# Chunked attention and a token/channel mixer on one core: batch 1's attention placed anew beside batch 0's feed-forward stage, with a subtracting softmax for every batch

## The chip, the cores and the metric

The kernel runs on one core of a Trainium2 chip. TensorE (PE) does the matrix products and transposes, VectorE (DVE) and ScalarE (ACT) read its results from eight PSUM banks, GpSimd (POOL) does small memsets and copies, and SyncE (SP) issues every DMA. The metric is the device time of one execution in microseconds, lower is better.

## What is computed

Shapes: 4 batches, 8 heads, 768 tokens, head dimension 64, 8 memory tokens, chunks of 32 queries that see 16 keys to the left and 8 to the right; rank 32, model width 512, hidden width 2048.

```python
for c in range(S // 32):                               # chunked attention
    k_full = concat(mem_k, k[l_start:r_end]); v_full = concat(mem_v, v[l_start:r_end])
    scores = scale * q_c @ k_full.T
    a = exp(scores - max(scores)); a = a / (sum(a) + 1e-9)
    out[c] = a @ v_full
x = out.transpose(0, 2, 1, 3).reshape(B, S, 512)
u = x + (x.T @ U @ V).T                                # low-rank token mixing
y = u + relu(u @ w_ch1) @ w_ch2                        # feed-forward over channels
```

The parameters U, V, w_ch1 and w_ch2 arrive as float64 and are decoded on the chip into a high and a low float32r part.

## The kernel before, in words

**Stages.** Batch 0's attention runs first, alone, while the weights begin to arrive. Then come the feed-forward stages of batches 0, 1, 2 and 3. Beside the stage of batch b runs the attention of batch b + 1, in pieces that are placed between the feed-forward's steps.

**The feed-forward.** A batch has 6 token tiles of 128, in two blocks of three, and the hidden width has 16 slices f. One unit is a block and a slice: `w1_step` is 12 matmuls of 128x384 (high weights by high u, low by high, high by low), followed by ACT's relu into `hh` and DVE's remainder `hl` (line 964); `w2_step` is 9 matmuls of 128x512 into three accumulators, the last three of which read `hl`. A batch thus has 32 units. In `both_blocks` (batch 0, lines 1019 to 1070) the two blocks take turns over the first `SPLIT` = 11 slices (units 0 to 21), since the weights are still being decoded; units 22 to 26 are block 0's slices 11 to 15, units 27 to 31 block 1's. Unit 26 ends with DVE's additions into `x` and the three stores of block 0 (line 973), unit 31 with those of block 1. The low parts of w1 for block 1's slices are read back from DRAM (`w1l`, line 378) two units ahead, into four buffers.

**The decoding.** `stream` (line 342) decodes 32 weight chunks on ACT and DVE; `advance` moves it on, two steps a unit, or as far as the next unit's weights need. `done` counts finished chunks; it reaches 32 at the start of unit 26. Its work space is `vbs[1]`, `vbs[2]` and two slots.

**Attention of one batch.** Three pairs T = 0, 1, 2 of token tiles. The pieces are: `k_part` and `q_part` (eight transposes each and ACT's copies into `kall` or `qt`), `s_part` (128 small matmuls into two PSUM banks, then the softmax in `s_weights` and the sums in `s_sums`), `t_part` (eight transposes of the weights and ACT's copies), `av_part` (128 small matmuls with the values in `vb`, then DVE's division into `x`). After the last pair come `collect` (12 matmuls with U), the replication (line 837) with a cast and a subtraction (lines 842, 843), six products with `v3` (line 858) and DVE's additions. `make_uT` (line 933) then turns three tiles of x for the next stage. `attention` is a generator: each `yield` ends a piece, and `place(n)` issues the next n.

**Order.** PE and SP keep the order in which the program issues (`manual_schedule`); DVE does so until unit 22 and ACT until unit 2; after that, and on POOL, the scheduler orders by priority. In `both_blocks`, `place(1)` is called at unit `2 * SPLIT - SOON` = 16 and `border()` twice in each of units 23 to 31, ahead of and behind the `w1_step`; what is left goes to `following` in unit 31. In the stages of batches 1 and 2, `STEPS` says at which slice a piece is placed.

**Loads of a batch's attention.** `loads` (line 421) is a generator too: k and q of pairs 0 and 1 with the memory values (17 steps), v of pair 0 (11), k and q of pair 2 (8), v of pairs 1 and 2. `serve(3)` issues three steps a unit; `need` issues what a piece lacks. v of a pair is eight loads of 98 or 112 KB, and some edges. For batch 1, pairs 0 and 1 use `vbs[0]`, so pair 1's load waits until `av_part(0)` is issued, and pair 2 uses `vbs[1]` once `done` is 32. For batches 2 and 3 pairs 0 and 2 use `vbs[0]`, pair 1 `vbs[1]`. Raw k, q, weights, x, `qt`, `pt` and `pT` share 23 slots.

**The softmax before.** Batch 0 (lines 591 to 595, 602 to 606): maximum on DVE, subtraction on DVE into `pt`, one exponential of 128x512 on ACT, sums on DVE. Batches 1 to 3 (lines 582 to 590): q is negated and scaled when it is copied, DVE takes the minimum, and ACT does eight exponentials of 128x64 that take it as bias and give the sum by their accumulator. A pair has two halves s, each so.

PSUM has three banks `ps_a` (attention, and block 1's accumulators until unit 21), two `ps_h` and three accumulators.

Of the kernel before, what the change touches and what calls it, by code (L numbers as in the profile page):

```python
# [1 line left out]

# [6 lines left out]
F32 = mybir.dt.float32  # L9
F32R = mybir.dt.float32r  # L10
BF16 = mybir.dt.bfloat16
AF = mybir.ActivationFunctionType
# [3 lines left out]
I32 = mybir.dt.int32  # L16
U32 = mybir.dt.uint32
NEG = -3.0e38
FAR = 3.0e38
NSLOT = 23  # L20
NVE = 1
ET = mybir.EngineType
# [14 lines left out]
NDEC = 3  # L37
RATE = 2
AHEAD = 2
SOON = 6  # L40
RATEL = 3
STEPS = [0, 4, 6, 8, 9, 10, 12, 13, 14, 15, 16, 17, 18, 19, 20, 23, 25, 26, 27, 28]


@with_exitstack
def chunk_attn_then_mixer_kernel(
# [324 lines left out]
    def advance(n):  # L371
        for _ in range(n):
            next(weights, None)
# [7 lines left out]
    def attention(b, xs):  # L381
# [30 lines left out]
        def fetch_v(T):  # L412
            if T == 0:
                clear_v()
            if T == 0 or T == (2 if b == 1 else 1):
                mem_v(v_home(T))
                yield
            yield from load_v(T)
            issued.add(("v", T))

        def loads():
            for T in range(2):
                yield from fetch(T, "kn", kn, k, LEFT)
                yield from fetch(T, "qn", qn, q, 0)
                if T == 0:
                    for g in range(2):
                        nc.sync.dma_start(out=mv[64 * g:64 * g + NM].rearrange("m (j d) -> m j d", d=D), in_=mvv[b, g])
                    yield
            yield from fetch_v(0)
            yield from fetch(2, "kn", kn, k, LEFT)  # L430
            yield from fetch(2, "qn", qn, q, 0)
            for T in (1, 2):
                while (done[0] < 2 * NF if v_home(T) is vbs[1] else "av0" not in issued):
                    yield "shut"
                yield from fetch_v(T)

        def need(*what):
            while what not in issued:
                assert next(feed[0], None) != "shut"
# [11 lines left out]
                )  # L451

        def v_home(T):
            return vbs[T if b == 0 else T // 2 if b == 1 else T % 2]

        def clear_v():
            for g in range(2):
# [73 lines left out]
        def q_part(T, h):  # L531
            psv = turn(qn.pop((T, h)))
            if front[0]:
                qt = const.tile([P, 2, NB, CK], F32, name="qt", tag=f"w1_{5 + (2 * T + h) % 3}")
            else:
                qt = slot([P, 2, NB, CK], F32, "qt")
            qts[T, h] = qt
            for q_ in range(2):
                to, src = qt[:, q_].rearrange("c i (n r) -> c r i n", r=2), psv[:, q_]
                if b > 0:  # L540
                    nc.scalar.mul(out=to, in_=src, mul=-scale)
                else:
                    (nc.vector.tensor_copy if T == 0 else nc.scalar.copy)(out=to, in_=src)

# [17 lines left out]
            return banks, psv  # L562

        def s_weights(T, banks, psv):
            if b > 0:
                rs = rss[T] = sm.tile([P, 2, 2, 2, 2], F32, name="rs", bufs=3)
            far = NEG if b == 0 else FAR
            for s in range(2):
                if T == 0:
                    nc.vector.memset(psv[s][0:CK, 0, :, :, NM:NM + LEFT], far)  # L570
                if T == NP - 1:
                    nc.vector.memset(psv[s][P - CK:P, 1, :, :, NW - 8:NW], far)
                if front[0]:
                    both = const.tile([P, 2, 512], F32, name="pt", tag=f"w2_{5 + 2 * T + s}")
                    pt, pT[T, s] = both[:, 0], both[:, 1].rearrange("c (j n) -> c j n", j=4)
# [3 lines left out]
                ptv = pt.rearrange("n (a w) -> n a w", w=NW)  # L579
                mx = sm.tile([P, 8], F32, name="mx", bufs=3)  # L580
                sc = banks[s].rearrange("n (a w) -> n a w", w=NW)
                if b > 0:
                    nc.vector.tensor_reduce(out=mx, in_=sc, axis=AX.X, op=ALU.min)  # L583
                    for a in range(8):
                        t, k_, g = a // 4, a // 2 % 2, a % 2
                        nc.scalar.activation(  # L586
                            out=ptv[:, a], in_=sc[:, a], func=AF.Exp, bias=mx[:, a:a + 1], scale=-1.0,
                            accum_out=rs[:, t, g, k_, s:s + 1],
                        )
                    continue  # L590
                nc.vector.tensor_reduce(out=mx, in_=sc, axis=AX.X, op=ALU.max)
                nc.vector.tensor_tensor(
                    out=ptv, in0=sc, in1=mx[:, :, None].broadcast_to([P, 8, NW]), op=ALU.subtract,
# [1 line left out]
                nc.scalar.activation(out=pt, in_=pt, func=AF.Exp, scale=scale)  # L595

        def s_sums(T):
            if b > 0:
                rs = rss[T]
            else:  # L600
                rs = rss[T] = sm.tile([P, 2, 2, 2, 2], F32, name="rs", bufs=3)
                for s in range(2):
                    nc.vector.tensor_reduce(
                        out=rs[:, :, :, :, s].rearrange("n t g k -> n t k g"),
                        in_=pts[T, s].rearrange("n (t k g w) -> n t k g w", t=2, k=2, g=2), axis=AX.X, op=ALU.add,
                    )
            nc.vector.tensor_scalar_add(out=rs, in0=rs, scalar1=1e-9)
            nc.vector.reciprocal(out=rs, in_=rs)

        def s_part(T):  # L610
            s_weights(T, *s_turn(T))
            s_sums(T)
# [162 lines left out]
        else:  # L775
# [2 lines left out]
            feed[0] = loads()  # L778
            yield
            place_memk()  # L780
            for T in two:
                for part, name in ((k_part, "kn"), (q_part, "qn")):
                    need(name, T)
                    for h in two:
                        part(T, h)
                    yield
            s_part(0)
            yield
            for s in two:
                t_part(0, s)  # L790
            yield
            need("v", 0)
            av_part(0)
            issued.add("av0")
            yield
            need("kn", 2)
            for h in two:
                k_part(2, h)
            yield
            s_part(1)  # L800
            yield
            need("qn", 2)
            for h in two:
                q_part(2, h)
            yield
            for s in two:
                t_part(1, s)
            yield
            s_part(2)
            yield  # L810
            need("v", 1)
            av_part(1)
            yield
            for s in two:
                t_part(2, s)
            yield
            if b == 1:
                while done[0] < 2 * NF:
                    advance(1)
                    more_w()  # L820
            need("v", 2)
            av_part(2)
            yield

        if b > 0:
# [193 lines left out]
    def both_blocks(pieces, following):  # L1019
# [11 lines left out]
        for n, (blk, f, where, begins, ends) in enumerate(units):  # L1031
# [15 lines left out]
                del w1ls[f]  # L1047
            if n == 2 * SPLIT - SOON:
                place(1)
            serve(RATEL)  # L1050
            if n > 2 * SPLIT:
                border()
            hid_ = w1_step(0, blk, f, w1l)
# [18 lines left out]
    def place(n):  # L1072
        for _ in range(n):
            next(gen[0], None)

    def serve(n):
        for _ in range(n):
            if next(feed[0], "shut") == "shut":
                return

    def border():
        place(1)

    def ffn(b, blk, pieces, following):
        prev = []
# [37 lines left out]
    feed = [iter(())]  # L1123
    for b in range(B):
        gen[0] = attention(b + 1, xs) if b + 1 < B else iter(())
        pcs = [STEPS.count(n) for n in range(2 * NF)]

        def last_turns(b=b):
            for _ in gen[0]:
                pass  # L1130
            yield from make_uT(b + 1, 0)

        turns = last_turns()

# [49 lines left out]
```

## Time and profile before

| | us |
|---|---|
| median of the 3 runs | 692.09 |
| the three runs | 693.47, 688.77, 692.09 |
| the profiled execution | 689.29 |
| its span, first to last instruction | 687.5 |
| mean granted TensorE clock | 0.99 |

| stretch of the profiled execution | from, to | length |
|---|---|---|
| batch 0, units 0 to 21, from about | 60, 154.65 | 94.7 |
| batch 0, units 22 to 31, with batch 1's attention | 154.65, 234.73 | 80.1 |
| batch 1's stage, with batch 2's attention | 234.73, 392.25 | 157.5 |
| batch 2's stage, with batch 3's attention | 392.25, 549.60 | 157.4 |
| batch 3's stage | 549.60, 682.50 | 132.9 |

Times in the profile are microseconds from the start of the span, unless marked ns. A line of a timeline has the start, the length, the engine, the line of the kernel, the operation, what it writes and reads with the shape, how many, and in brackets how long the engine stood idle before and what ended that. SPq is SyncE's queue: its lines are the issues of transfers. In a line of operations by source the three durations are the least, the median and the greatest in ns. Matmuls are pipelined, so their lengths overlap: the distance from one start to the next is their cost.

### The profile page before, as it was taken

The page shows a single profiled execution, that of the slowest core. Times are in us where ns is not written, and L with a number is a line of the kernel's source. Part 1 is how long each engine was busy: PE and PEld are TensorE (multiplying, and loading weights), DVE is VectorE, ACT ScalarE, POOL GpSimd, SP SyncE. Part 2 cuts the span into 40 slices and gives each one's busy share as a digit, 9 for nine tenths or more (in the row PEclk, how much of TensorE's full clock was granted, in tenths as well). Part 3 has the DMA queues.
Part 4 walks back from the last instruction along what each step waited for, and adds up shares of the span by engine and source line. Part 5 has one row for each costly group of instructions (what it writes and reads, how often), then busy time and mean ns, then how long its engine had stood idle before and what let it go on. Part 6 is the DMA issues. An engine that isn't in the chain of part 4 may idle for free.

```text
span 687.5 us, 14945 instructions
## 1 busy us (share of the span) xinstructions
PE 658.2 (96%) x6284; PEld 576.0 (84%) x6284; DVE 246.7 (36%) x488; ACT 241.9 (35%) x792; POOL 10.1 (1%) x35
## 2 busy tenths in 40 slices
PE   7687999999879999999999999999999999999997
PEld 4457999988666799989988999898888899989996
DVE  5768666876322511132224211233223221131111
ACT  4646555677553223445211122535311111111110
POOL 2100000000000000000000000000000000000000
PEclk9999999999999999999999999999999999999999
DMA  8788444844082285427121185525220142204211
GB/s 229 165 239 298 144 154 154 251 112 129 8 218 46 87 211 127 110 60 183 48 63 50 57 225 113 145 67 154 76 63 32 30 138 67 70 23 145 65 47 46
DMA packets 122997, 79.88 MB, mean 116 GB/s; under 512 B 86994, under 2 KB 102482, under 8 KB 122930
## 3 DMA queue, kind: packets, MB, share of 16 engines
q1 hardware_dynamic: 122930, 78.93, 41.4%
q8 instruction: 49, 0.80, 0.5%
q14 instruction: 18, 0.15, 0.1%
HBM read 67.24 MB, written 10.49 MB: 113 GB/s over the span
## 4 chain that ended last, share of the span: by engine, by line
PE 86%; SPq 6%; DMA 2%; DVE 2%; ACT 2%; issue 1%; ACTq 0%; DVEq 0%
PE ps_h L957 38%; PE acc L1005 23%; PE acc L1010 12%; SPq L481 3%; PE ps_a L500 2%; PE ps_a L634 2%; PE ps_a L1005 2%; PE ps_a L557 2%; PE ps_a L941 1%; ACT pt L586 1%; PE ps_a L619 1%; PE ps_a L1010 1%; DMA rw<-in_moe_w_ch_dram 1%; PE ps_a L660 1%; DMA vb<-in_v_dram 1%
## 5 line engine op out<-in xcount | busy, mean ns | idle before, releaser
L964 DVE SCALAR_TENSOR_TENSOR hl<-ps_h,hh 128x384 fp32r<-128x384 f32 x127 | 70.7, 557 | 315.4 <-ACT hh L963 315.3
L957 PE MATMUL ps_h<-uh,w1h 128*128 128x384 f32 x508 | 174.7, 345 | 0.5 <-issue 0.5
L957 PE MATMUL ps_h<-ul,w1h 128*128 128x384 f32 x508 | 171.0, 338 | 0.0
L963 ACT ACTIVATE hh<-ps_h 128x384 fp32r<-128x384 f32 x127 | 63.2, 497 | 292.6 <-PE ps_h L957 292.6
L1005 PE MATMUL acc<-w,hh 128*128 128x512 f32 x606 | 158.4, 397 | 0.0
L1005 PEld LDWEIGHTS acc<-w,hh 128*128 128x128 f32 x606 | 111.8, 188 | 24.2 <-issue 2.5
L957 PE MATMUL ps_h<-uh,w1l 128*128 128x384 f32 x508 | 108.7, 334 | 3.4 <-DVE w1l L333 3.4
L957 PEld LDWEIGHTS ps_h<-uh,w1h 128*128 128x128 f32 x508 | 96.1, 189 | 3.8 <-issue 1.5
L957 PEld LDWEIGHTS ps_h<-ul,w1h 128*128 128x128 f32 x508 | 96.0, 189 | 2.4 <-issue 0.7
L957 PEld LDWEIGHTS ps_h<-uh,w1l 128*128 128x128 f32 x508 | 89.8, 188 | 3.7 <-DVE w1l L333 3.7
L1010 PE MATMUL acc<-w,hl 128*128 128x512 f32 x303 | 86.3, 393 | 0.0
L1010 PEld LDWEIGHTS acc<-w,hl 128*128 128x128 f32 x303 | 57.3, 189 | 12.6
L586 ACT ACTIVATE pt<-ps_a,mx 128x64 f32<-128x64 f32 x144 | 43.4, 355 | 17.3 <-DVE mx L583 15.4
L586 ACT ACTIVATION_READ_ACCUMULATOR pt<-ps_a,mx 128x1 f32 x144 | 35.6, 248 | 0.0
L521 ACT COPY kall<-ps_a 128x256 f32<-128x256 f32 x40 | 17.1, 427 | 30.8 <-PE ps_a L500 30.8
L971 DVE TENSOR_TENSOR x<-acc,x 128x512 f32<-128x512 f32 x24 | 15.2, 681 | 22.9 <-PE acc L1010 19.1
L1005 PE MATMUL acc<-w2last,hh 128*128 128x512 f32 x90 | 23.1, 392 | 0.0
L643 DVE TENSOR_TENSOR x<-ps_a,rs 128x256 f32<-128x256 f32 x44 | 15.8, 415 | 11.3 <-PE ps_a L634 9.0
L1005 PEld LDWEIGHTS acc<-w2last,hh 128*128 128x128 f32 x90 | 16.8, 188 | 3.4
L557 PEld LDWEIGHTS ps_a<-kall,qt 64*32 64x32 f32 x1344 | 16.1, 105 | 3.7 <-issue 3.3
L557 PE MATMUL ps_a<-kall,qt 64*32 64x64 f32 x1344 | 18.5, 225 | 0.2 <-issue 0.2
L1005 PE MATMUL ps_a<-w,hh 128*128 128x512 f32 x66 | 17.0, 393 | 0.0
(205 smaller groups left out, 590.7 us busy)
## 6 DMA issues: line engine op xcount, KB each, us to landing
w1l<-w1ld SPq DMA_DIRECT2D x101, 256.0 KB
rw<-in_moe_w_ch_dram SPq DMA_DIRECT2D x14, 512.0 KB
out_dram<-x SPq DMA_DIRECT2D x24, 256.0 KB
vb<-in_v_dram SPq DMA_DIRECT2D x56, 98.0 KB
raw<-in_moe_w_ch_dram SPq DMA_DIRECT2D x20, 256.0 KB
qn<-in_q_dram SPq DMA_DIRECT2D x36, 128.0 KB
rw<-in_moe_w_ch_dram SPq DMA_DIRECT2D x16, 256.0 KB
w1ld<-w1l SPq DMA_DIRECT2D x16, 256.0 KB
```

The costliest lines, as they stand in the source:

```text
L481: nc.sync.dma_start(out=vt[r0:r0 + NW - NM, n0:n1, D * j:D * j + D], in_=bass.AP(rows.tensor, rows.offset, [[step, count], [CK * step, n1 ...
L500: nc.tensor.transpose(out=psv[:, p, r, :], in_=half[:, r, 2 * p:2 * p + 2, :].rearrange("n h d -> n (h d)"), identity=ident,)
L521: copy(out=kt[:, p, :, :, m:m + w], in_=psv[:, q_])
L557: nc.tensor.matmul(out=psv[s][CK * i:CK * i + CK, t, p % 2, p // 2, :], lhsT=qt[p // 2][rows, p % 2, NI * t + i, :], rhs=kall[rows, NB * ( ...
L586: nc.scalar.activation(out=ptv[:, a], in_=sc[:, a], func=AF.Exp, bias=mx[:, a:a + 1], scale=-1.0, accum_out=rs[:, t, g, k_, s:s + 1],)
L643: nc.vector.tensor_tensor(out=x[:, 4 * D * g:4 * D * g + 4 * D].rearrange("n (j d) -> n j d", d=D), in0=psv[g][:, t], in1=rs[:, t, g].rear ...
L957: nc.tensor.matmul(out=ph[:, :TOK], lhsT=w[:, c, :], rhs=u[c], start=(m == 0), stop=(m + 1 == len(parts)),)
L963: nc.scalar.activation(out=hh, in_=ph[:, :TOK], func=AF.Relu)
L964: nc.vector.scalar_tensor_tensor(out=hl, in0=ph[:, :TOK], scalar=0.0, in1=hh.bitcast(F32), op0=ALU.max, op1=ALU.subtract,)
L971: nc.vector.tensor_tensor(out=x, in0=bank, in1=x, op=ALU.add)
L1005: nc.tensor.matmul(out=acc[tt], lhsT=h[:, sl], rhs=w, start=(begins and m == 0), stop=False,)
L1010: nc.tensor.matmul(out=acc[tt], lhsT=hl[:, sl], rhs=w2h[f], start=False, stop=ends is not None)
```

## The change

1. The softmax of batches 1 to 3 is done as batch 0's: plain copy of q, maximum, subtraction, one exponential with the scale, sums on DVE.
2. The pieces of the attention of batches 1 to 3 come in another order: scores of pair 0 right behind k of pair 1, k of pair 2 ahead of the first weighting.
3. For batch 1 the values of pair 1 go to `vbs[1]` and wait for `done` = 32; those of pair 2 go to `vbs[0]` and wait for `av_part(0)`: the way of batches 2 and 3.
4. In batch 0's stage loading starts at unit 14 (`SOON` 8), with three steps a unit until unit 21 and six (`RATES`) from unit 22.
5. The 18 borders place as `PLAN` says: one piece at each of the first 13, then 2, 1, 2, 2, 4. `make_uT(1, 0)` is chained to batch 1's attention and placed by the same list instead of by `following` in unit 31.

In the new order the borders of units 23 to 31 hold (ahead of `w1_step` / behind it): k0 / q0; k1 / s0; q1 / t0; k2 / av0; s1 / q2; t1 / s2; av1 / t2 and av2; collect / replication and three `v3` products; the other three and the first turn / the other two turns. Before they held: k0 / q0; k1 / q1; s0 / t0; av0 / k2; s1 / q2; t1 / s2; av1 / t2; av2 / collect; replication / three products, with the rest in `following`.

```diff
-FAR = 3.0e38
-SOON = 6
+SOON = 8
 RATEL = 3
+RATES = 6
+PLAN = [1] * 13 + [2, 1, 2, 2, 4, 1, 1]
...
         def fetch_v(T):
-            if T == 0 or T == (2 if b == 1 else 1):
+            if T < 2:
                 mem_v(v_home(T))
...
             for T in (1, 2):
-                while (done[0] < 2 * NF if v_home(T) is vbs[1] else "av0" not in issued):
+                while (done[0] < 2 * NF if T == 1 else "av0" not in issued):
                     yield "shut"
...
         def v_home(T):
-            return vbs[T if b == 0 else T // 2 if b == 1 else T % 2]
+            return vbs[T if b == 0 else T % 2]
...
                 if b > 0:
-                    nc.scalar.mul(out=to, in_=src, mul=-scale)
+                    nc.scalar.copy(out=to, in_=src)
...
         def s_weights(T, banks, psv):
-                if b > 0:
-                    nc.vector.tensor_reduce(out=mx, in_=sc, axis=AX.X, op=ALU.min)
-                    for a in range(8):
-                        t, k_, g = a // 4, a // 2 % 2, a % 2
-                        nc.scalar.activation(
-                            out=ptv[:, a], in_=sc[:, a], func=AF.Exp, bias=mx[:, a:a + 1], scale=-1.0,
-                            accum_out=rs[:, t, g, k_, s:s + 1],
-                        )
-                    continue
                 nc.vector.tensor_reduce(out=mx, in_=sc, axis=AX.X, op=ALU.max)
                 nc.vector.tensor_tensor(
                     out=ptv, in0=sc, in1=mx[:, :, None].broadcast_to([P, 8, NW]), op=ALU.subtract,
...
                 nc.scalar.activation(out=pt, in_=pt, func=AF.Exp, scale=scale)
...
         def s_sums(T):
-            if b > 0:
-                rs = rss[T]
-            else:
...
+            for s in range(2):
+                nc.vector.tensor_reduce(
+                    out=rs[:, :, :, :, s].rearrange("n t g k -> n t k g"),
+                    in_=pts[T, s].rearrange("n (t k g w) -> n t k g w", t=2, k=2, g=2), axis=AX.X, op=ALU.add,
+                )
...
+            for what, args in (
+                (turn_in, (k_part, "kn", 0)), (turn_in, (q_part, "qn", 0)), (turn_in, (k_part, "kn", 1)),
+                (s_part, (0,)), (turn_in, (q_part, "qn", 1)), (weights_in, (0,)), (turn_in, (k_part, "kn", 2)),
+                (weigh, (0,)), (s_part, (1,)), (turn_in, (q_part, "qn", 2)), (weights_in, (1,)), (s_part, (2,)),
+                (weigh, (1,)), (weights_in, (2,)),
+            ):
+                what(*args)
+                yield
+            weigh(2)
             yield
...
-            serve(RATEL)
+            serve(RATEL if n < 2 * SPLIT else RATES)
...
+    at = [0]
+
     def border():
-        place(1)
+        place(PLAN[at[0]])
+        at[0] += 1
...
         gen[0] = attention(b + 1, xs) if b + 1 < B else iter(())
+        if b == 0:
+            gen[0] = chain(gen[0], make_uT(1, 0))
...
         def last_turns(b=b):
             for _ in gen[0]:
                 pass
-            yield from make_uT(b + 1, 0)
+            if b > 0:
+                yield from make_uT(b + 1, 0)
```

`turn_in` needs the load and turns both halves, `weights_in` is `t_part` of both halves, `weigh` needs v and is `av_part`.

More of the change, by code (lines that the diff above doesn't have):

```diff
@@ L1 @@
 from contextlib import ExitStack
+from itertools import chain
 import concourse.bass as bass
@@ L564, in s_weights @@
         def s_weights(T, banks, psv):
-            if b > 0:
-                rs = rss[T] = sm.tile([P, 2, 2, 2, 2], F32, name="rs", bufs=3)
-            far = NEG if b == 0 else FAR
             for s in range(2):
                 if T == 0:
-                    nc.vector.memset(psv[s][0:CK, 0, :, :, NM:NM + LEFT], far)
+                    nc.vector.memset(psv[s][0:CK, 0, :, :, NM:NM + LEFT], NEG)
                 if T == NP - 1:
-                    nc.vector.memset(psv[s][P - CK:P, 1, :, :, NW - 8:NW], far)
+                    nc.vector.memset(psv[s][P - CK:P, 1, :, :, NW - 8:NW], NEG)
                 if front[0]:
@@ L597, in s_sums @@
         def s_sums(T):
-            if b > 0:
-                rs = rss[T]
-            else:
[L601 to L606, printed above, removed]
+            rs = rss[T] = sm.tile([P, 2, 2, 2, 2], F32, name="rs", bufs=3)
+            for s in range(2):
[3 more added lines that the diff above has]
+                )
             nc.vector.tensor_scalar_add(out=rs, in0=rs, scalar1=1e-9)
@@ L780, in attention, with turn_in, weigh, weights_in @@
             place_memk()
[L781 to L822, printed above, removed]
+            def turn_in(part, name, T):
+                need(name, T)
+                for h in two:
+                    part(T, h)
+            def weigh(T):
+                need("v", T)
+                av_part(T)
+                issued.add(f"av{T}")
+            def weights_in(T):
+                for s in two:
+                    t_part(T, s)
+            for what, args in (
[7 more added lines that the diff above has]
+            weigh(2)
             yield
```

## The prediction

> **What bounds the kernel now.** I read the page's busy shares first, then the windows of the stages, then TensorE's (PE's) timeline where it is not full, and last the queue that it waits for.
>
> ```profile
> span 687.5 us, 14945 instructions
> PE 658.2 (96%) x6284; PEld 576.0 (84%) x6284; DVE 246.7 (36%) x488; ACT 241.9 (35%) x792; POOL 10.1 (1%) x35
> ```
>
> The windows have, after the stretch and its length, the busy microseconds of PE, PE's weight loads, DVE, ACT and POOL, then the granted clock, the DMA share and GB/s. These four are batch 1's feed-forward stage with batch 2's attention in it, batch 2's with batch 3's, batch 3's with none, and the stretch at the end of batch 0's stage where batch 1's attention runs.
>
> ```profile
> 234.73:392.25 157.52, 157.52 (x1558) 140.48 (x1557) 39.17 (x80) 48.13 (x186) 2.03 (x6) 1.00 0.40 104
> 392.25:549.60 157.35, 157.35 (x1558) 140.35 (x1557) 39.20 (x80) 48.11 (x186) 0.61 (x2) 1.00 0.40 104
> 549.60:682.50 132.90, 132.90 (x679) 121.14 (x679) 23.21 (x42) 17.35 (x35) 0.00 (x0) 1.00 0.24 72
> 154.65:234.73 80.08, 70.48 (x1072) 56.91 (x1071) 32.99 (x69) 39.55 (x171) 2.02 (x6) 0.96 0.35 86
> ```
>
> In the first three PE is never idle: whatever ACT, DVE or a transfer does there is under PE's stream, and a cheaper softmax can give nothing. The fourth is the only place that this change touches and where PE waits. What it should last follows from the others. Batch 3's stage is 32 units (a `w1_step` and a `w2_step`): 132.90 / 32 = 4.15 us each. Attention with its turning costs PE 157.4 - 132.9 = 24.5 us where it is hidden. The stretch holds nine `w1_step` and ten `w2_step`, 9.5 units: 9.5 x 4.15 + 24.5 = 63.9 us. It lasts 80.08, so 16.2 us is lost: the ceiling of the gain.
>
> Where it is lost, by PE's timeline (start, length, the idle time before it in brackets):
>
> ```profile
> 171.77 0.45 PE L619 MATMUL ps_a<-ident,pt 128*128 128x128 f32 x2
> ...
> 174.63 0.33 PE L619 MATMUL ps_a<-ident,pt 128*128 128x128 f32 x1 [0.65 <-ACT pt L586]
> ...
> 175.90 2.31 PE L1005 MATMUL acc<-w,hh 128*128 128x512 f32 x6
> ...
> 179.41 1.70 PE L634 MATMUL ps_a<-vb,pT 64*32 64x64 f32 x128
> ...
> 191.95 0.27 PE L500 MATMUL ps_a<-ident,qn 128*128 128x128 f32 x1
> 195.21 0.55 PE L500 MATMUL ps_a<-ident,qn 128*128 128x128 f32 x3 [2.98 <-DMA qn<-in_q_dram]
> ...
> 197.02 1.82 PE L619 MATMUL ps_a<-ident,pt 128*128 128x128 f32 x8
> ...
> 206.75 1.54 PE L634 MATMUL ps_a<-vb,pT 64*32 64x64 f32 x126 [1.05 <-ACT pt L586]
> 208.83 0.44 PE L957 MATMUL ps_h<-uh,w1h 128*128 128x384 f32 x1 [0.54 <-issue]
> ...
> 211.03 1.03 PE L619 MATMUL ps_a<-ident,pt 128*128 128x128 f32 x8
> 211.82 1.63 PE L1005 MATMUL acc<-w,hh 128*128 128x512 f32 x6
> ...
> 214.06 1.28 PE L634 MATMUL ps_a<-vb,pT 64*32 64x64 f32 x95
> ...
> 225.49 0.86 PE L858 MATMUL ps_a<-g,v 96*128 96x512 f32 x3
> ...
> 228.92 1.85 PE L941 MATMUL ps_a<-ident,x 128*128 128x128 f32 x12
> ```
>
> Undisturbed, eight transposes take 211.82 - 211.03 = 0.79 and a `w2_step` 214.06 - 211.82 = 2.24. Pair 0's weight transposes run from 171.77 to 175.90 (4.13), trickling behind ACT's exponentials; pair 2's q transposes from 191.95 to 197.02 (5.07), waiting for a load. After both, the clock is down:
>
> ```profile
> 176.00:180.00 4.00, 4.00 (x53) 2.81 (x58) 1.64 (x3) 1.88 (x5) 0.00 (x0) 0.58 0.00 0
> ...
> 196.00:198.00 2.00, 1.66 (x9) 1.50 (x10) 0.25 (x1) 1.21 (x4) 0.00 (x0) 0.77 1.06 287
> 198.00:200.00 2.00, 2.00 (x9) 2.00 (x9) 0.00 (x0) 1.18 (x2) 0.00 (x0) 0.50 1.00 230
> ```
>
> The first drop loses 0.42 x 4 = 1.7 us, the second 0.23 x 2 + 0.5 x 2 = 1.5.
>
> Why that load is late, by SyncE's queue:
>
> ```profile
> 154.91 9.28 SPq L308 DMA_DIRECT2D w1ld<-w1l  x2
> ...
> 169.42 0.45 SPq L406 DMA_DIRECT2D qn<-in_q_dram  x1
> 188.70 3.01 SPq L973 DMA_DIRECT2D out_dram<-x  x3
> ...
> 192.24 1.54 SPq L406 DMA_DIRECT2D qn<-in_q_dram  x3
> ...
> 208.10 0.38 SPq L489 DMA_DIRECT2D vb<-in_v_dram  x1
> ```
>
> SyncE goes in program order. At 169.87 it meets the stores of batch 0's first block (line 973), which wait until `w2_step` of unit 26 is done, and stands until 188.70. Behind them are three of pair 2's q loads and all of pairs 1 and 2's v, issued from 192.24 to 208.5 at about 0.5 us apiece (three in 1.54), with the DMA engines full (shares 1.06 and 1.00 above).
>
> **The change part by part.**
>
> *Loads ahead of the stores.* Loading starts at unit 14 instead of 16, three steps a unit, six from unit 22. The list has 36 steps up to pair 2's q: 8 x 3 = 24 by unit 21, 30 at unit 22, 36 at unit 23; before, unit 23 had 24 and unit 26 had 33. So all of pair 2's q is issued before the stores, by about 169 us, where its first load went (the 169.42 row) as step 33. Pair 1's v now goes to `vbs[1]` and no longer waits for `av_part(0)` but for the last weight chunk (`done` 32, which unit 26 forces before it serves): its memory rows and four of its eight loads still pass ahead of the stores. The q wait goes: 5.07 - 0.79 = 4.3 us off PE, and the second clock drop of 1.5 with it. The raw k and q tiles are held earlier, while raw weights still fill the slots. I count nothing for it: a wait for a slot falls where SyncE stands anyway (9.28 us in the 154.91 row); what it costs without that cover is rival 4.
>
> *Softmax.* Per half pair, out go 8 exponentials with their 8 accumulator reads; in come a subtraction, one exponential and a sum. Batch 0 has these rows already:
>
> ```profile
> L592 DVE TENSOR_TENSOR pt<-ps_a,mx x3: 691/692/693, 16.5 to 28.8; 128x512 f32<-128x512 f32 x3
> L595 ACT ACTIVATE pt<-pt x6: 629/631/653, 15.6 to 29.5; 128x512 f32<-128x512 f32 x6
> L603 DVE TENSOR_REDUCE rs<-pt x6: 674/678/679, 17.7 to 34.6; 128x8 f32<-128x512 f32 x6
> L583 DVE TENSOR_REDUCE mx<-ps_a x18: 680/686/693, 169.8 to 480.3; 128x8 f32<-128x512 f32 x18
> L586 ACT ACTIVATE pt<-ps_a,mx x144: 303/352/417, 170.5 to 485.2; 128x64 f32<-128x64 f32 x144
> L586 ACT ACTIVATION_READ_ACCUMULATOR pt<-ps_a,mx x144: 192/245/311, 170.8 to 485.4; 128x1 f32 x144
> ```
>
> ACT loses 8 x (0.35 + 0.25) = 4.8 us of records per half (overlapping ones) and gains 0.63; DVE gains 0.69 + 0.68. A pair's weights are ready after two maxima and two subtractions (4 x 0.69 = 2.8) and one exponential (0.63): 3.4 us after the scores. From pair 0's scores to its transposes the new order lays a `w2_step`, a q part and a `w1_step`: about 5.2 us. So that trickle goes: 4.13 - 0.79 = 3.3 us, and the first clock drop, 1.7. Pair 1 has a `w1_step` and a q part (3.0), and its second half is wanted 0.4 later: it meets 3.4, and I count a wait of 0.2, where the late q load hid it until now. Before the 206.75 row the second weighting waits for banks that pair 2's exponentials still read; a subtraction gives them back within 1.5 us, under the `w2_step` between: 1.05 and the issue gap of 0.54 after it, 1.6 gained.
>
> *Order and places.* Scores 0 follow k of pair 1 after one `w1_step` (half of 4.15), while ACT copies keys for 2.25 (the first and the last of ten copies, below): 0.3 lost. Weight transposes and weighting of pair 2 come together, without a `w2_step` between: PE waits for ACT's copy (row below, 0.59) and about 0.2 of hand-over: 0.8 lost. The replication and the first three `v3` products come together too, with the cast and the subtraction below between them (0.58 + 0.69 + 0.2): 1.5 lost. In return the next three products stand a `w2_step` later, so the six, which now take 228.92 - 225.49 = 3.4, take 1.6, and 0.4 is lost where the first turn meets the last bank: 1.4 gained.
>
> ```profile
> 162.30 0.39 ACT L521 COPY kall<-ps_a 128x256 f32<-128x256 f32 x1
> ...
> 164.23 0.32 ACT L525 COPY kall<-ps_a 128x48 f32<-128x48 f32 x1
> ```
>
> ```profile
> L622 ACT COPY pT<-ps_a x18: 582/590/691, 176.7 to 490.6; 128x512 f32<-128x512 f32 x18
> L842 ACT CAST g<-ps_a x3: 582/582/583, 223.6 to 520.0; 96x512 fp32r<-96x512 f32 x3
> L843 DVE TENSOR_TENSOR g<-ps_a,g x3: 689/689/689, 224.2 to 520.6; 32x512 fp32r<-32x512 f32 x3
> ```
>
> *V behind the stores.* Still behind them: pair 1's other four loads, then pair 2's ten, with a w1l fetch between. From the end of unit 26, SyncE needs 3.4 us until the stores are out (3.01, and 0.4 for the additions before), 2.5 for the first five issues and 5.5 for eleven more: done at +5.9 and +11.4. The landing is known from the chain of waits of that stretch:
>
> ```profile
> 199.02 5.10 DMA vb<-in_v_dram
> ```
>
> With 5.1 us pair 1's v is there at +11.0 and pair 2's at +16.5. PE wants them at +10.9 (scores 1.5 as in the 206.75 row, `w1_step` 2.1, q 0.8, transposes 0.8, `w1_step` 2.1, scores 1.5, `w2_step` 2.1) and, a weighting, a `w1_step`, transposes and the copy later, at +16.1. A tie, with less traffic than before (17 transfers instead of about 30): I take 0, with bounds 0 and 3.
>
> *Batches 2 and 3.* Order, softmax and the q copy change in full stages; DVE rises from 39 to about 47 us of 157. I take 0; bounds -0.5 to +1.
>
> The sum: 4.3 + 1.5 + 3.3 + 1.7 + 1.6 + 1.4 = 13.8 won, 0.2 + 0.3 + 0.8 + 1.5 = 2.8 lost: **11.0 us won**. Of the ceiling of 16.2, 5 stays. The profiled execution took 689.29 (687.5 and 1.8 around the span), so 678.3. The three runs shown reach from 688.77 to 693.47, median 692.09, and the four executions together average 690.9. I set the forecast between, at **680**.
>
> On the clock: the drop at 176 follows 4.1 us in which PE never stood longer than 0.65 and was about half busy. [...]
>
> **Rivals.**
>
> 1. *The v transfers end last.* For it: the tie above, and DMA shares of 1.06 and 1.00 in the rows at 196 and 198. Against: less is queued. A wait of 3 us and a clock drop of 1.7 bring the gain to 6.3: about 685. Chance 0.17.
> 2. *DVE's softmax is late.* The stretch then has 33 + 6 x 1.37 = 41 us of DVE work in about 69, and the last weight chunks and three x additions stand in its in-order queue ahead of the maxima. If each of three pairs is 1.5 us late, with one clock drop, 6.2 are given back: gain 4.8, about 686. Against: DVE is busy in 33 of the 80 us now. Chance 0.09.
> 3. *The other side: DVE delays `hl` in batches 1 and 2's stages.* The hidden-layer remainder (line 964) stands behind subtraction and sum in DVE's queue, and PE's third pass needs it. Twelve halves bring 12 x 1.37 = 16.4 us; if two thirds come out on PE, the 11.0 is gone, and if all do, the time is 5.4 worse: 696. Against: DVE is idle three quarters of these stages, and each remainder has a whole step before it is used. Chance 0.06.
> 4. *The early loads don't get ahead*, because raw slots or SyncE's waits on weight saves hold them until the stores. Then only softmax and order pay: 3.3 + 1.7 + 1.6 + 1.4 - 2.8 = 5.2, about 686. For it: SyncE stood 9.28 us on two such saves at 154.91. Against: unit 26's loads still passed ahead of the stores (169.42). Chance 0.06.
>
> **How the numbers follow.** My forecast has 0.62; it holds 675 (nearly the whole ceiling of 16.2) to 684. Reaching to rivals 1, 2 and 4 gives 675 to 688, leaving out the slower side. About 1%, 7 us, is what a measurement of this kernel can tell from no change: below 685.2 is faster. That is nearly all of my case, half of rival 1 and some of 2 and 4, and the runs' own scatter favours neither side: 0.74 faster, 0.19 the same, 0.07 slower.
>
> **What would show it.** Right: in PE's timeline no idle time for the loading of qn and none for pt at the first transposes; no window with a granted clock near 0.5 between unit 23 and batch 1; the stretch near 69 us; three q loads ahead of the stores in SyncE's queue; new waits of about 0.8 before the last weighting and 1.5 before the `v3` products; the stages of batches 1 to 3 as long as before. Wrong: PE idle at line 634 for vb, waits at line 619 for pt over 1 us, or any of the three full stages longer by over 1 us.

## The result and the profile after

The changed kernel takes 685.51 us (median of 20 runs, 682.86 to 690.52) against 692.54 us (688.77 to 695.17) for the kernel before beside it: ratio 0.9907, 95% interval 0.9888 to 0.9926, or 7.0 us. The forecast was 680, a gain of 11.0 us, with the range 675 to 688. Direction and range held; the gain is two thirds of the sum.

The profiled execution took 690.52, the longest of the 20, so single terms are read from it and the total is not. In the full stages nothing moved. These windows are batch 0's end with batch 1's attention, and the stages of batches 1 and 2; the columns are as in the prediction.

```profile
span 688.7 us, 14707 instructions
...
157.66:235.90 78.24, 69.62 (x1072) 58.13 (x1071) 40.18 (x80) 28.70 (x83) 2.02 (x6) 0.91 0.27 72
235.90:393.44 157.54, 157.54 (x1558) 140.60 (x1557) 47.02 (x92) 37.55 (x96) 2.02 (x6) 1.00 0.39 104
393.44:550.60 157.16, 157.16 (x1556) 140.26 (x1556) 46.66 (x92) 37.53 (x96) 0.61 (x2) 1.00 0.40 104
```

DVE rose from 39.2 to 47.0 us in batch 1's stage and ACT fell from 48 to 38, under a PE that is never idle: 157.54 us against 157.52.

Inside the first window PE's timeline is the one forecast up to 198 us (lines of the changed kernel: 502 turns k and q, 559 scores, 606 weight transposes, 621 weighting, 926 `w1_step`, 974 and 979 `w2_step`).

```profile
174.34 1.03 PE L606 MATMUL ps_a<-ident,pt 128*128 128x128 f32 x8
175.13 1.63 PE L974 MATMUL acc<-w,hh 128*128 128x512 f32 x6
...
189.75 1.03 PE L502 MATMUL ps_a<-ident,qn 128*128 128x128 f32 x8
190.62 0.60 PE L606 MATMUL ps_a<-ident,pt 128*128 128x128 f32 x4
191.69 0.66 PE L606 MATMUL ps_a<-ident,pt 128*128 128x128 f32 x4 [0.47 <-ACT pt L585]
...
198.07 1.48 PE L621 MATMUL ps_a<-vb,pT 64*32 64x64 f32 x128
203.12 0.48 PE L926 MATMUL ps_h<-uh,w1h 128*128 128x384 f32 x1 [3.57 <-issue]
...
206.91 1.77 PE L606 MATMUL ps_a<-ident,pt 128*128 128x128 f32 x8
208.65 0.45 PE L621 MATMUL ps_a<-vb,pT 64*32 64x64 f32 x16
209.36 1.21 PE L621 MATMUL ps_a<-vb,pT 64*32 64x64 f32 x89 [0.27 <-ACT pT L609]
212.34 0.65 PE L621 MATMUL ps_a<-vb,pT 64*32 64x64 f32 x23 [1.77 <-issue]
...
224.27 0.98 PE L827 MATMUL ps_a<-g,v 96*128 96x512 f32 x3 [1.40 <-DVE g L812]
...
228.31 0.65 PE L910 MATMUL ps_a<-ident,x 128*128 128x128 f32 x4 [0.32 <-DVE x L829]
```

Pair 0's transposes take 0.79 (4.13 before), pair 2's q 0.87 (5.07 before), and the second weighting at 198.07 waits neither for banks nor for v. What is new are two waits put down to "issue", that is, to nothing that these rows show: 3.57 us ahead of unit 29's `w1_step`, and 1.77 us in the middle of one group of 128 matmuls, of which 105 had run. After each the clock is at half:

```profile
204.00:206.00 2.00, 2.00 (x8) 2.00 (x8) 0.00 (x0) 0.00 (x0) 0.00 (x0) 0.50 0.00 0
...
214.00:216.00 2.00, 2.00 (x6) 1.59 (x5) 0.44 (x2) 0.00 (x0) 0.00 (x0) 0.50 0.00 0
```

SyncE's queue has the loads where the change puts them: pair 2's q at 152.44 (the prediction had about 169), half of pair 1's v at 171.53, both ahead of the stores.

```profile
152.44 2.33 SPq L408 DMA_DIRECT2D qn<-in_q_dram  x4
...
171.53 3.36 SPq L483 DMA_DIRECT2D vb<-in_v_dram  x4
186.50 1.53 SPq L942 DMA_DIRECT2D out_dram<-x  x3
```

### The profile page after: what moved, and what is told of

Read it like the earlier page. It is cut to its first block, busy times and chain, and to the rows that moved or that the text cites. A ratio compares the mean times of both kernels' runs of the same rounds, so it can differ in the third digit from the quotient of the medians.

```text
span 688.7 us, 14707 instructions
## 1 busy us (share of the span) xinstructions
PE 659.2 (96%) x6280; PEld 578.0 (84%) x6284; DVE 269.7 (39%) x524; ACT 208.8 (30%) x522; POOL 10.1 (1%) x35
## 4 chain that ended last, share of the span: by engine, by line
PE 88%; SPq 4%; DMA 3%; DVE 2%; issue 1%; ACT 0%; DVEq 0%
PE ps_h L926 39%; PE acc L974 24%; PE acc L979 12%; PE ps_a L974 2%; PE ps_a L502 2%; PE ps_a L621 2%; DMA rw<-in_moe_w_ch_dram 2%; PE ps_a L559 2%; SPq L483 2%; PE ps_a L910 1%; PE ps_a L606 1%; PE ps_a L979 1%; PE ps_a L647 1%; DMA raw<-in_moe_w_ch_dram 1%; DMA qraw<-in_q_dram 1%
## 5 line engine op out<-in xcount | busy, mean ns | idle before, releaser
L974 PE MATMUL acc<-w,hh 128*128 128x512 f32 x606 | 158.9, 398 | 0.0
L585 ACT ACTIVATE pt<-pt 128x512 f32<-128x512 f32 x24 | 14.8, 633 | 22.8 <-DVE pt L582 22.8
L543 ACT COPY qt<-ps_a 128x256 f32<-128x256 f32 x36 | 11.4, 410 | 17.9 <-PE ps_a L502 17.9
```

The source lines that it names most:

```text
L974: nc.tensor.matmul(out=acc[tt], lhsT=h[:, sl], rhs=w, start=(begins and m == 0), stop=False,)
```

## The experiments

My first theory for the missing 4 us: PE gets its own instructions late while the DMA engines are full behind the stores. The second, formed from the second profile: PE gets them in blocks of 16 KB, and dense groups outrun the blocks. The size is read from the changed kernel's page: its row q8, marked instruction, has 0.80 MB in 49 packets, while PE has 6280 matmuls and 6284 weight loads, 12,564 instructions, or 256 a packet.

```profile
PE 659.2 (96%) x6280; PEld 578.0 (84%) x6284; DVE 269.7 (39%) x524; ACT 208.8 (30%) x522; POOL 10.1 (1%) x35
...
q8 instruction: 49, 0.80, 0.5%
```

The trace also holds the time of each of these packets. In batch 3's stage, where PE is never idle, five of them start 24.5 to 25.4 us apart (560.39 to 659.88), and PE has 250 to 261 matmuls and weight loads between two starts, so the packets follow PE's instructions. At the first wait one starts at 199.91, 0.36 us after PE ran dry; it lands at 201.85, and PE goes on at 203.12. The next starts at 209.80 and lands at 211.04, and PE goes on at 212.34. In the windows 199.9 to 201.9 and 209.8 to 211.8 each stands alone in its queue's row (packets, MB, share of 16 engines' time in those 2 us):

```profile
q8 instruction: 1, 0.02, 6.1%
...
q8 instruction: 1, 0.02, 3.9%
```

In the profiles of all kernels here, each of the 19 issue waits of 0.49 us or more in this stretch ends 1.25 to 1.70 us after such a packet has landed (1.27 and 1.30 in these two, 1.26 and 1.28 in the first profile of the kernel before). Between the two waits lie 125 matmuls and as many weight loads, about one packet. So the traces show what PE waited for; the runs test why it comes late and what that costs.

The table has the median, the ratio to the kernel before beside it, and two parts of the profiled execution: the time at which batch 1's k is first turned, and the stretch from there to batch 1's stage.

| kernel | median us (runs) | ratio, 95% interval | k turned at | stretch us |
|---|---|---|---|---|
| before | 692.54 (20) | | 155.5 | 79.2 |
| before, again | 690.88 (10) | 0.9968, 0.9937 to 0.9999 | 157.2 | 79.4 |
| changed | 685.51 (20) | 0.9907, 0.9888 to 0.9926 | 158.2 | 77.7 |
| changed, again | 685.22 (10) | 0.9917, 0.9890 to 0.9945 | 154.2 | 76.2 |
| changed, old softmax | 687.13 (12) | 0.9936, 0.9905 to 0.9967 | 156.8 | 75.7 |
| before, new softmax | 689.78 (12) | 0.9980, 0.9958 to 1.0003 | 157.2 | 77.8 |
| before, new transfers | 688.49 (12) | 0.9956, 0.9936 to 0.9976 | 158.1 | 78.7 |
| changed, v ahead | 681.14 (6) | 0.9852, 0.9823 to 0.9881 | 157.3 | 70.8 |
| changed, more loads | 687.03 (10) | 0.9930, 0.9903 to 0.9956 | 158.9 | 76.6 |
| changed, tail apart | 683.16 (6) | 0.9884, 0.9856 to 0.9913 | 156.8 | 71.1 |
| changed, groups apart | 684.87 (6) | 0.9874, 0.9832 to 0.9916 | 157.7 | 69.3 |
| changed, v ahead and tail apart | 683.64 (6) | 0.9870, 0.9828 to 0.9913 | 159.7 | 68.5 |
| changed, shifted | 678.76 (6) | 0.9789, 0.9753 to 0.9825 | 155.9 | 68.4 |
| before, shifted | 687.96 (12) | 0.9965, 0.9938 to 0.9991 | 155.6 | 75.6 |

The kernel before against itself gave 0.9968: differences under about 0.4% are not resolved here.

**The changed kernel again.**

> The changed kernel once more, for a second profile and for the spread of its times. My theory: what is missing of the forecast gain of 11 us is lost while the DMA engines are full behind the stores (188 to 201 us), because TensorE then gets its own instructions late: the idle time shown as issue, 3.57 us ahead of a w1_step and 1.77 us in the middle of 128 small matmuls, and two windows at half clock after it. It expects a time of 685.5 (683 to 689), idle time shown as issue again between 190 and 215, of another size than 3.57 and 1.77, and a front part (to unit 0's second matmuls, 62.1 here and 59.1 before, with the same order of instructions) that scatters by some us. Rival A (the changed loads slow the front part): the front part is again 3 us longer than before's. Rival B (the waits are for data, v or low weights): the idle times come back at the same places with the same sizes, within 0.3 us.

```profile
199.15 0.48 PE L926 MATMUL ps_h<-uh,w1h 128*128 128x384 f32 x1 [3.57 <-issue]
...
208.20 0.42 PE L621 MATMUL ps_a<-vb,pT 64*32 64x64 f32 x23 [2.58 <-issue]
```

Both waits are back at the same instructions, the second again with 23 matmuls of its group left; the first has the same size, the second not. Against rival A, batch 1's k was turned at 154.2 here, 4 us earlier than in the first profile: the front part scatters with one and the same program. Rival B's places came back, but only one of its two sizes; that the waits are not for data is shown by the packets' times above and by the shifted kernel below. The same size of the first wait spoke against my theory, and I formed the second.

**The kernel before again.** The same program as before, for its scatter.

> The kernel before once more, for a second profile of it. If its first profile (689.29, one of its fastest) is typical: the stretch from the first turning of batch 1's k to batch 1's stage again takes 79.2 us within 1, and the issue waits in it are again under 0.6 us each. If the kernel before loses time in the same way as the changed one, only not in that execution: a longer stretch, 80 to 83 us, with an issue wait of 1.5 us or more.

```profile
209.16 0.44 PE L957 MATMUL ps_h<-uh,w1h 128*128 128x384 f32 x1 [1.28 <-issue]
```

```profile
198.00:200.00 2.00, 2.00 (x17) 2.00 (x15) 0.03 (x1) 1.74 (x5) 0.00 (x0) 1.00 0.93 223
```

The stretch is 79.4 us against 79.2, so the profile that I forecast from was typical of it in length. It was not in every part: after the wait for pair 2's q, 2.41 us here, the window from 198 is at 1.00 where the first profile has 0.50, so the `w1_step` behind it is not slowed in each execution. Whether the second drop that the prediction books came earlier here is not shown; the stretch's mean clock is 0.96 in both profiles. The kernel before has issue waits too, 1.28 and 0.77 us in this profile, above the 0.6 that I expected of it, but of no size that explains the 4 us.

**Undoing the softmax, and its parts alone.**

```diff
 old_softmax: the changed kernel, with FAR, s_sums and the q copy of the one before, and
+                if b > 0:
+                    nc.vector.tensor_reduce(out=mx, in_=sc, axis=AX.X, op=ALU.min)
+                    for a in range(8):
...
+                            out=ptv[:, a], in_=sc[:, a], func=AF.Exp, bias=mx[:, a:a + 1], scale=-1.0,
...
+                    continue
 only_softmax: the kernel before, with s_weights, s_sums and the q copy of the changed one
 only_transfers: the kernel before, with v_home, fetch_v, loads, SOON = 8 and RATES = 6 of the changed one
```

> The changed kernel with the former softmax for batches 1 to 3 (minimum, eight exponentials with accumulators, no sums on DVE); order, places and transfers as changed. If the softmax pays as forecast: pair 1's exponentials take about 6 us after the scores with 3 us of cover (a w1_step and a q part), so its transposes wait about 3 us where 0.5 was seen; pair 0's have 5.2 us of cover and wait about 1; the second weighting waits 1 for its banks; with a clock drop of 1.7 the time is 5 to 7 us above the changed kernel's, about 691. If the softmax is worth nothing (all of the gain is the transfers'): within 1.5 us of the changed kernel.

> The kernel before with the new softmax alone; order, places and transfers as before. By my sum: pair 0's transposes 3.3, the clock drop after them 1.7, the second weighting 1.6 are won, the wait for pair 2's q and its clock drop stay: 4 to 6 us below the kernel before, about 687.5. If the softmax pays only together with the earlier loads: within 1.5 us of the kernel before.

> The kernel before with the new transfers alone: loading from unit 14, six steps from unit 22, pair 1's v in the second buffer; softmax, order and places as before. By my sum the wait for q (4.3) goes, but pair 1's transposes then meet exponentials of about 6 us with 3 us of cover, so that 2 to 3 us come back, and the clock drop may stay: 1.5 to 4 us below the kernel before, about 690. If the transfers are the whole gain: 6 to 7 us below, about 686.

By the medians the undone softmax lost 1.9 us, where 5 to 7 were forecast. The new softmax alone gained 1.7 against a forecast of 4 to 6; its interval reaches 1.0003, so this is not told from no gain. The new transfers alone gained 3.0, inside their 1.5 to 4. Where each meets the other's wait shows in PE's timelines, in this order:

```profile
193.43 2.06 PE L622 MATMUL ps_a<-ident,pt 128*128 128x128 f32 x8 [1.71 <-ACT pt L589]
...
211.81 0.43 PE L637 MATMUL ps_a<-vb,pT 64*32 64x64 f32 x24 [1.76 <-issue]
```

```profile
192.88 1.79 PE L500 MATMUL ps_a<-ident,qn 128*128 128x128 f32 x7 [2.43 <-DMA qn<-in_q_dram]
...
206.82 0.33 PE L942 MATMUL ps_h<-uh,w1h 128*128 128x384 f32 x1 [2.67 <-issue]
```

```profile
199.15 1.97 PE L620 MATMUL ps_a<-ident,pt 128*128 128x128 f32 x8 [2.09 <-ACT pt L587]
```

With early loads and the old softmax, pair 1's transposes wait 1.71 and 2.09 for the exponentials that the late q had covered, as the prediction had it. But the 3.57 us ahead of unit 29's `w1_step` are gone with the old softmax, and only the second issue wait is left, 1.76: that the waits for exponentials pull the dense groups apart is a likely reason, not a shown one, why undoing the softmax cost less than forecast. With the new softmax alone the q wait stays at 2.43, and an issue wait of 2.67 stands where the kernel before has 0.54 and 1.28, there behind waits for banks of 1.05 and 1.32 that are gone here: as one wait went, the next was longer.

**Loads moved away, loads added.**

```diff
 v_ahead
             if n > 2 * SPLIT:
                 border()
+            if n == 26:
+                serve(15)
 extra_loads
+            if n == 29:
+                for m in range(4):
+                    spare = slot([P, 512], I32, "spare")
+                    nc.sync.dma_start(out=spare, in_=w2[m * P:(m + 1) * P, 0:512])
```

> The changed kernel, with fifteen load steps served behind the second border of unit 26: all of pair 1's and pair 2's v is issued ahead of block 0's stores, PE's order is the same. Theory 1 (PE's instructions come late because the DMA engines are full from 188 to 201 us): the issue waits of 3.57 ahead of a w1_step and of 1.8 to 2.6 in the second of the two weightings shrink to under 1 us together, and the half clock after them goes: 679 to 682. Theory 2 (PE gets its instructions in blocks of 16 KB, 256 of them, 3.57 us after it asks, however busy the DMA engines are, and two groups of 128 weight loads and 128 matmuls that lie 2.2 us apart outrun that): both waits stay, within 0.5 us, and the time is that of the changed kernel within 1.5 us, 684 to 687.

> The changed kernel with four more loads of 256 KB each into slots that nothing reads, issued in unit 29 right behind pair 2's v, so that the DMA engines stay full some 5 us longer, from 201 to about 206 of the first profile; PE's order is the same. Theory 1 (full DMA engines delay PE's instructions): the issue wait ahead of that w1_step grows from 3.57 by 2 to 5 us, and the time by 2 to 5. Theory 2 (a fixed time per block of instructions): 3.57 again, and the time within 1.5 us of the changed kernel's 685.4.

PE's waits and the windows around the first, v ahead and then more loads:

```profile
200.90 0.33 PE L926 MATMUL ps_h<-uh,w1h 128*128 128x384 f32 x1 [2.17 <-issue]
```

```profile
198.00:200.00 2.00, 0.73 (x75) 0.75 (x61) 1.93 (x6) 0.37 (x1) 0.00 (x0) 1.00 0.04 8
...
202.00:204.00 2.00, 2.00 (x8) 2.00 (x7) 0.00 (x0) 0.00 (x0) 0.00 (x0) 0.50 0.04 8
```

```profile
204.06 0.48 PE L926 MATMUL ps_h<-uh,w1h 128*128 128x384 f32 x1 [3.85 <-issue]
...
213.17 0.42 PE L621 MATMUL ps_a<-vb,pT 64*32 64x64 f32 x23 [2.58 <-issue]
```

Neither theory holds alone. With the DMA engines nearly idle (0.04) the first wait is still 2.17, so load is not needed for it; but it shrank by 1.4, the second went, and the median lies some 4 us below the changed kernel's, which the second theory had not allowed. Filling the engines for longer added 0.3 to the first wait and left the second at the 2.58 of the repetition; the first theory had 2 to 5 us. So a block can be 2.17 us late with idle engines, and load made it up to 1.7 us later in these profiles. The late packet itself took 1.2 us with v ahead and 1.2 to 1.9 in the profile with more loads and the two of the changed kernel, so it is late mostly because it starts late. When PE asks for a block is in no row: that it comes 3.57 us after the asking was my estimate from the size of the first wait. The clock dropped to 0.50 here (the row at 202) after a wait of 2.17.

**Places.**

```diff
-PLAN = [1] * 13 + [2, 1, 2, 2, 4, 1, 1]
+PLAN = [1] * 17 + [6]                      (tail_apart, and ahead_tail with v_ahead's line)
+PLAN = [1] * 12 + [0, 1, 1, 1, 1, 7]       (groups_apart)
```

> The changed kernel with one piece at each of the first 17 borders and the rest at the last: transposes and weighting of pair 2 with a w2_step between, the replication ahead of the last w1_step and all v3 products behind it, as in the kernel before. Theory 2: the issue wait in pair 2's weighting (1.8 to 2.6) shrinks to under 0.7, that of 3.57 ahead of the w1_step stays; with 0.3 and 1.4 won on the copy and the replication and about 1.5 lost at the tail, the time is 2 to 4 us below the changed kernel: 681.5 to 683.5. Theory 1: the issue waits are as before and the time is within 1.5 us of 685.4.

> The changed kernel with the pieces behind scores 2 one border later each: nothing ahead of unit 29's w1_step, the weighting of pair 1 behind it, transposes and weighting of pair 2 at unit 30's two borders, collect ahead of unit 31's w1_step and all the rest behind it. Between two groups of 128 matmuls then lies at least a w1_step and a w2_step (4.2 us). The transfers are as changed. Theory 2: no issue wait over 0.7 us is left, nor a clock near 0.5; at the tail the replication's 1.4 and about 2 for the v3 products and turns are uncovered; 4 to 7 us below the changed kernel: 678.5 to 681.5. Theory 1: the waits stay where the DMA engines are full, whatever PE runs then, and the time is within 1.5 us of 685.4 or above it for the uncovered tail.

> The changed kernel with both edits that won: all v ahead of the stores, and one piece at each of the first 17 borders with the rest at the last. If their gains are two parts of the same loss: v_ahead's 681.1 less the copy's and the replication's 1.7, plus 1.5 at the tail, so 680 to 682. If they add (4.3 and 2.2 off 685.4): 678 to 680. In both cases the issue wait ahead of unit 29's w1_step stays at about 2.2 us.

The first waits left over, in this order (tail apart, groups apart, and both edits; of the last also its wait at the front):

```profile
201.15 0.48 PE L926 MATMUL ps_h<-uh,w1h 128*128 128x384 f32 x1 [3.02 <-issue]
```

```profile
202.24 0.33 PE L621 MATMUL ps_a<-vb,pT 64*32 64x64 f32 x11 [1.23 <-issue]
```

```profile
40.92 0.26 PE L621 MATMUL ps_h<-vb,pt 64*32 64x64 f32 x1 [5.89 <-issue]
...
202.99 0.34 PE L926 MATMUL ps_h<-uh,w1h 128*128 128x384 f32 x1 [1.89 <-issue]
```

With the tail apart the second wait is gone and the first stays, as the second theory had it, and the median is within its forecast. With the groups apart one wait of 1.23 is left, where the theory allowed 0.7, and the stretch is 69.3 us, but the median, 684.87, missed its 678.5 to 681.5 (one of its six executions took 816.11 at a mean granted clock of 0.75, for which nothing here gives a cause; the other five lie between 676.76 and 685.99). Its profile shows two places outside the stretch where time went: a front wait of 2.86 us (more on it next), and batch 2's stage, 159.1 us instead of 157.3, with an issue wait of 1.05 at 480 us. So a full stage had such a wait too, in this execution. Both edits together gave the stretch of 68.5 that they should, and a median of 683.64, above v ahead alone: the profile has 5.89 us of issue wait in batch 0's own weighting, at 41 us, where the order of instructions is the same in all kernels here except the two shifted ones. That front wait was 0.7 to 5.9 us in the eleven profiles of unshifted kernels that show it (0.68 and 0.82 in the two of the kernel before, 3.81 and 1.18 in those of the changed one), so the medians of these three do not rank them.

**The block tested by itself.**

```diff
-START = 12
+START = 8
+SHIFT = [68]
...
+        while warm[0] and SHIFT:
+            for _ in range(SHIFT.pop()):
+                nc.tensor.matmul(out=ps[:, 0:16], lhsT=busy[:, 0:P], rhs=busy[:, 0:16], start=True, stop=True)
```

> The changed kernel with 128 more instructions in TensorE's stream at the very start (four of the warming products fewer, 68 products of 16 columns more, all on zeros and before the first data), so that every later instruction lies half a block of 256 further on; nothing else is changed. If PE waits for blocks of 256 instructions: the wait ahead of unit 29's w1_step moves into the middle of a group of 128 matmuls and shrinks from 3.57 to about 1.3 (the block is asked for half a group and a w2_step, 3.7 us, before it is needed instead of 1.5), the second one shrinks or goes, and the time falls by 2 to 6 us, to 679.5 to 683.5. If the waits belong to these places of the program or to the loads alone: both stay where they are, and the time is 684 to 687.

> The kernel before with the same 128 more instructions at the very start of PE's stream; nothing else is changed. It tells how much of the 678.8 of the shifted changed kernel belongs to the shift alone. If the shift mends what the change itself did (the kernel before loses only 0.5 to 1.3 us at a time to its instructions): 688 to 692, so that with the same shift the change is worth 10 to 13 us, as the sum of the prediction had it. If the shift mends something that both kernels lose alike: 682 to 686, and the change is worth 4 to 7 us with it as without.

```profile
195.85 0.86 PE L625 MATMUL ps_a<-vb,pT 64*32 64x64 f32 x64
197.74 0.85 PE L625 MATMUL ps_a<-vb,pT 64*32 64x64 f32 x64 [1.03 <-issue]
...
201.99 2.02 PE L625 MATMUL ps_a<-vb,pT 64*32 64x64 f32 x128 [0.24 <-ACT pT L613]
```

```profile
155.92:224.30 68.38, 64.58 (x1070) 54.31 (x1071) 39.80 (x79) 28.59 (x83) 2.03 (x6) 1.00 0.29 78
```

The wait moved by exactly the 128 instructions that were put in: from behind the group's last matmul to behind its 64th. It shrank from 3.57 to 1.03, the second went, the clock stays at 1.00, and the median is 678.76 us, a little below its forecast, ratio 0.9789: the best kernel of this study, and it computes what the changed one does with 128 useless instructions more. The stretch is 9.3 us shorter than in the first profile of the changed kernel, and the two rows account for it: 4.3 are the waits (3.57 + 1.77 - 1.03), 5.0 are PE's busy time (69.62 against 64.58), at a granted clock of 0.91 against 1.00. The same shift leaves the kernel before at 0.9965, hardly further from 1 than its repetition, with a median of 687.96, just under its forecast of 688 to 692.

## Why the prediction was right in direction and short in size

- *What bounds the kernel* held: the full stages gave nothing (term taken as 0: +0.02 and -0.19 us), and what the shifted kernel's profile gains on the first of the kernel before lies in the one stretch where PE waits (68.4 us against 79.2).
- *Loads ahead of the stores* held: pair 2's q part 0.87 instead of 5.07, and no drop after it. *Softmax* held: 0.79 instead of 4.13, no wait for banks; pair 1's new wait was 0.47, I had 0.2.
- *Order and places* held: replication 1.40 (I had 1.5), the turn's bank 0.32 (0.4). For the copy the profile shows 0.27 at half clock where I had 0.8.
- *V behind the stores*, rival 1, did not happen: no wait of PE for `vb`. Nor did the others: 0.47 was the one wait for the softmax, the full stages kept their length, and the q loads got ahead of the stores.
- The failed step is the sum itself: it lacked a term for PE's own instructions. I had read the issue gap of 0.54 as part of the wait for banks and booked it as won. In the changed kernel scores, weighting, transposes and weighting follow so closely that PE needs its next block before it has come, 3.57 and 1.77 to 2.58 us late, each followed by a stretch at half clock. Of the two drops that I booked as won (3.2 us) the change made two others.
- With the blocks moved off the dense place the stretch is as long as the sum has it: 68.4 us, and 79.2 - 11.0 = 68.2. That is partly luck. The shift took 3.6 us out of the stretch of the kernel before too (75.6; its profile has no issue wait of 0.49 us or more there and no drop after pair 0's transposes), so that by the two shifted profiles the change is worth 75.6 - 68.4 = 7.2 us. By the ratios of the two it is worth (0.9965 - 0.9789) x 692 = 12.2 us, and by their medians 687.96 - 678.76 = 9.2. The 11.0 lies among these; the runs do not fix it better.

Open is why the block after a late one comes late too at some places (1.77 to 2.58 us in three profiles of this order) and not in the kernel with v ahead, whose order is the same. The packets' times narrow it: in the three its packet started only 6.4 to 6.7 us after PE had gone on from the first wait, with v ahead 1.5 us after. Open is also how much of the shifted kernels' narrow spread (676.35 to 679.85 for the changed one) is the front wait, which their profiles do not show. Two profiles of the changed kernel show a stretch only 1.5 to 3 us shorter than before, while the medians differ by 7.0. Between the profiles of the two repetitions (685.00 and 692.25 us) 3.0 us lie ahead of the stretch, where PE's order is the same in both, and 3.1 in it. So the runs do not show where all of the 7.0 comes from.

## What to carry to other kernels

Price PE's instructions like a transfer: count those between two waits, and distrust a place where groups of many tiny matmuls come within a few microseconds of each other, even with all data there; here the groups of 128 had waits of 3.57 and 1.77 us behind and inside them. An idle time that the profile puts down to "issue" was the sign of it in these runs, above all in the middle of a group (1.77 us behind 105 of 128 matmuls); moving it by half a block with useless instructions early in the stream is a cheap test, and here it was worth about as much as the change itself (685.51 to 678.76). My sum was 11.0 us here, new waits of 3.57 and 1.77 came, and the medians differ by 7.0: I would take a sum of removed waits as an upper bound until the next resource has been priced.

## What the runs showed of the hardware that was not expected

In these traces PE's instructions come by the queue marked instruction in packets of 16 KB, one per 256 instructions (49 packets for 12,564 instructions in the changed kernel, 50 for the 12,691 of the shifted one), and where PE waited for one it went on 1.25 to 1.70 us after the packet had landed. A group of 128 weight loads and 128 matmuls, as many instructions as a packet has, ran in 1.48 us (the row at 198.07). Ahead of unit 29's `w1_step` the next packet was 2.17 us late with v ahead, at a DMA share of 0.04 in the window in which PE ran dry, and 1.89 with v ahead and the tail apart; it was 3.02 to 3.85 us late in the changed kernel's two profiles, with more loads and with the tail apart, at shares of 0.87 to 1.00 in that window.

The granted clock fell to 0.50 after single waits of 2.17 to 3.85 us, and after one of 1.77 that followed another drop. It stayed at 1.00 after waits of 1.03 and 1.40 (shifted). Where no window gives it, the steps behind a wait do: the matmuls of a `w1_step` start 0.17 us apart at 1.00 and 0.32 at 0.50 (the changed kernel, 557 and 204 us). Behind the 1.89 with v ahead and the tail apart they start 0.17 apart, and behind the 1.76 with the old softmax the `w2_step` takes 2.27 us, as the 2.24 undisturbed; behind the 1.71 for exponentials with the old softmax they start 0.32 apart. So the length of one wait does not decide it in these runs.
